# Postmix of an fp32 attention by 128 keys instead of 112: three whole parts a tile, half parts of two tiles side by side

## The chip, the cores and the metric

One core of one Trainium2 chip runs the whole program. The metric is the device time of one execution in microseconds. TensorE (PE; its weight loads are shown as PEld), VectorE (DVE), ScalarE (ACT), GpSimd (POOL) and SyncE (SP, which issues nearly all DMAs) run side by side and wait for each other by semaphores.

## What is computed

An attention over 4 batches, 12 heads, 448 tokens and 64 dimensions a head, whose heads are mixed before and after the softmax (premix by `w_pre`, postmix by `w_post`), and then two MLPs of 768 to 2048 to 768 over the 1792 tokens.

```python
scores = scale * np.matmul(q, k.transpose(0, 1, 3, 2))
scores = np.einsum('bhij,hg->bgij', scores, w_pre)
scores = scores - np.max(scores, axis=-1, keepdims=True)
attn = np.exp(scores)
attn = attn / (np.sum(attn, axis=-1, keepdims=True) + 1e-09)
attn = np.einsum('bhij,hg->bgij', attn, w_post)
return np.matmul(attn, v).astype(np.float32)
```

All of the attention is in fp32. Each fp32 matmul is two instructions on TensorE, each with a weight load of its own.

## The kernel before

The batches go in two groups of two: attention of a group, then both MLPs for it, then the other group. The MLPs split their operands in high and low fp32r parts and are not touched.

Within a group a batch's 448 rows of queries are 45 tiles of 10 rows (the last of 8), 90 tiles a group, in 8 chunks of 11 or 12 tiles. A tile has 10 rows times 12 heads = 120 rows of scores, by 448 keys. Two neighbouring tiles are a pair, and `slot(m)` writes out by hand the order of one pair's turn: 45 slots a group, each with the stages of several pairs:

- at its head, `keep(2m-1)` (the copy of the last pair's second tile), `soft(m+1)` (exponentials on ACT, L233), `premix(m+2)` (four matmuls on 64x64 quarters of the array, L217) and `top(m+2)` (maxima on DVE, L224);
- at its places A, B or C, up to three visits of `score` (L178, again 64x64 quarters), which are planned ahead of each chunk; some slots have none;
- `invert(m+1)` (reciprocals of the sums, DVE, L241 and L242), `postmix(2m)` with `keep(2m)`, `scale(m+1)` for both tiles (the post weights times the reciprocals, POOL, L251), in some slots `values` of a chunk (L293), then `postmix(2m+1)`.

`postmix(i)` takes the exponentials of a tile as weights, in JC = 4 parts of JP = 112 keys, and streams the scaled post weights `w2s` (12 heads times 10 rows = 120 columns). Its four results stand side by side in one bank, 112 partitions by 480 columns. `keep(i)` copies them into the chunk's tile `a` (keys, parts, heads, rows): even tiles on ACT (L278), odd tiles on DVE (L280). `values(c)` multiplies a chunk's `a` with V, over the same four parts, the two heads of a pair side by side: each matmul has 64 weight columns and writes one half of the output's partitions. The output banks `bo` are two, `w2s` tiles three, exponential tiles `p` four, `a` tiles two.

At the end of a group's slots `closing` runs the values of the last chunk. Beside the last ten slots of a group, steps of the next stage run on ACT, DVE and POOL (L585, L587 in the first group, L838, L842 in the second), and in the second group POOL also adds up weights (L492).

Of the kernel before, what the change touches and what calls it, by code (L numbers as in the profile page):

```python
# [7 lines left out]
F32 = mybir.dt.float32  # L8
# [8 lines left out]
RI = 10  # L17
# [51 lines left out]
def attention_mlp_kernel(ctx: ExitStack, tc, qT, kT, v, w_pre, w_post, mask, w1_in, w1_out, w2_in, w2_out, outT):  # L69
    nc = tc.nc  # L70
    B, _, _, S = kT.shape
    H, D = 2 * kT.shape[1], kT.shape[2] // 2
    JC, JP = v.shape[1], v.shape[2]
    DM = H * D
    P = 128
    KC = DM // P
    NF = w1_in.shape[0]
    G = H
    CH = chunks_of(S)
    CN = max(n for _, n, _, _ in CH)  # L80
# [16 lines left out]
    def bank(tag, name):  # L97
        return ps.tile([128, 512], F32, tag=tag, name=name)
# [5 lines left out]
    sh = ctx.enter_context(tc.tile_pool(name="sh", bufs=1))  # L104
# [25 lines left out]
    class Attention:  # L130
        def __init__(self, gi):
            self.gi = gi
            self.batches = list(range(gi * NB, gi * NB + NB))
            self.chunks = [(b, ci) for b in self.batches for ci in range(len(CH))]
            self.tiles, self.first, self.tb = [], [], []
            for c, (b, ci) in enumerate(self.chunks):
                r0, n, nt, nl = CH[ci]
                self.first.append(len(self.tiles))
                self.tiles += [(c, t, RI if t < nt else nl) for t in range(nt + (nl > 0))]
            self.first.append(len(self.tiles))  # L140
            self.n = -(-len(self.tiles) // 2)
            self.live, self.ss, self.aa, self.ap, self.xr = {}, {}, {}, None, None
            self.ks, self.n_raw, self.raw, self.at, self.late = None, 0, None, {}, False
            if gi == 0:
                self.first_opening()
            self.plan()
# [98 lines left out]
        def scale(self, m, a):  # L245
            if 2 * m + a >= len(self.tiles):
                return
            c, t, ni = self.tiles[2 * m + a]
            pts, rz = self.live["r", m]
            w2s = sh.tile([P, G * RI], F32, tag="w2s", name=f"w2s{self.gi}_{m}_{a}", bufs=3)  # L250
            nc.gpsimd.tensor_scalar(  # L251
                w2s[:, :G * ni].rearrange("p (g i) -> p g i", g=G), w2f[:, a, :, :ni], rz[:, a:a + 1], 1.0,
                op0=ALU.mult, op1=ALU.mult)
            self.live["w", 2 * m + a] = pts[a], w2s

        def postmix(self, i):
            if i >= len(self.tiles):
                return
            c, t, ni = self.tiles[i]
            pt, w2s = self.live.pop(("w", i))  # L260
            o = bank("bo", f"ps_o{self.gi}_{i}")
            for q in range(JC):
                nc.tensor.matmul(  # L263
                    o[:JP, q * G * ni:(q + 1) * G * ni], lhsT=pt[:, q * JP:(q + 1) * JP],
                    rhs=w2s[:, :G * ni], start=True, stop=True)
            self.live["o", i] = o

        def keep(self, i):
            if i >= len(self.tiles):
                return  # L270
            c, t, ni = self.tiles[i]
            if t == 0:
                self.aa[c] = self.ap.tile([JP, JC, G, CN], F32, tag="a", name=f"a{self.gi}_{c}", bufs=2)
            o = self.live.pop(("o", i))
            dst = self.aa[c].rearrange("p c g i -> p (c g) i")[:, :, t * RI:t * RI + ni]
            src = o[:JP, :JC * G * ni].rearrange("p (c i) -> p c i", i=ni)
            if i % 2 == 0:
                nc.scalar.activation(dst, src, AF.Copy)  # L278
            else:
                nc.vector.tensor_copy(dst, src)  # L280


        def values(self, c, vs, tag="bm"):
            b, ci = self.chunks[c]
            r0, n, _, _ = CH[ci]
            done = []
            for v in vs:
                xo = bank(tag, f"ps_v{self.gi}_{c}_{v}")
                for k in range(PAIRS):
                    for q in range(JC):  # L290
                        for e in range(2):
                            g = 2 * (v * PAIRS + k) + e
                            nc.tensor.matmul(  # L293
                                xo[e * D:(e + 1) * D, k * n:(k + 1) * n], lhsT=self.v[:, q, g, :],
                                rhs=self.aa[c][:, q, g, :n], start=(q == 0), stop=(q == JC - 1))
                done.append(xo)
            if self.xr is None:
                self.xr = sh.tile([P, KC, T], F32, tag="xr", name=f"xr{self.gi}")
            c0 = (b % NB) * S + r0
            for v, xo in zip(vs, done):  # L300
                dst = self.xr[:, v * PAIRS:(v + 1) * PAIRS, c0:c0 + n]
                src = xo[:, :PAIRS * n].rearrange("p (k i) -> p k i", i=n)
                nc.vector.tensor_copy(dst, src)
# [82 lines left out]
        def slot(self, m):  # L386
            work = self.at.get(m, [])

            def on(fn, k, *args):
                if 0 <= k < self.n:  # L390
                    fn(k, *args)

            def do(name, which=slice(None)):
                for fn, args in [w for w in work if w[0].__name__ == name][which]:
                    fn(*args)
            for k in self.fetches.get(m, ()):
                self.fetch(k)
            for name in ("fetch_k", "fetch_q", "fetch_v"):
                do(name)
            if 1 <= m <= self.n:  # L400
                self.keep(2 * m - 1)
            on(self.soft, m + 1)
            on(self.premix, m + 2)
            on(self.top, m + 2)
            visits = [w for w in work if w[0].__name__ == "score"]
            places = {0: "", 1: "B" if self.late else "A", 2: "BC" if self.late else "AC"}.get(
                len(visits), "AB" + "C" * len(visits))
            self.late = "C" in places

            def visit(place):  # L410
                for at, (fn, args) in zip(places, visits):
                    if at == place:
                        fn(*args)

            visit("A")
            on(self.invert, m + 1)
            if 0 <= m < self.n:
                self.postmix(2 * m)
                self.keep(2 * m)
            visit("B")  # L420
            on(self.scale, m + 1, 0)
            on(self.scale, m + 1, 1)
            for fn, args in work:
                if fn.__name__ == "values":
                    fn(*args, "by" if m % 2 else "bm")
            if 0 <= m < self.n:
                self.postmix(2 * m + 1)
                if m == self.n - 1:
                    self.keep(2 * m + 1)
            visit("C")  # L430

        def run(self, ap, behind, beside=None):

            self.ap = ap
            self.v = ap.tile([JP, JC, G, D], F32, tag="v", name=f"v{self.gi}")
            if self.gi == 0:
                for step in self.ahead():
                    step()
            behind, at = list(behind), self.n - 9
            for m in range(self.n + 1):  # L440
                if m < self.n:
                    self.slot(m)
                if beside:
                    beside(ap, m)
                if at <= m < at + KC:
                    behind.pop(0)()
                for _ in range(2):
                    if m >= at + KC and len(behind) > 2 * (self.n - m) + 1:
                        behind.pop(0)()
            return behind  # L450
# [294 lines left out]
    class Blocks(Mlps):  # L745
# [122 lines left out]
        def beside(self, ap, i):  # L868

            j, o = (i - 1) // 4, (i - 1) % 4  # L870
            todo = self.beside_todo
            if i < 1:
                return
            if o == 3 and 2 <= j < len(todo) + 2:
                self.store_sums(j - 2)
            if o == 1 and j < len(todo):
                prepare(*todo[j], 0, [ap.tile([P, 2, HW], F32, tag=f"pr{r}", name=f"pr{r}_{j}", bufs=3) for r in range(2)])
            if 1 <= j <= len(todo):
                prepare(*todo[j - 1], 1, eng=nc.gpsimd, ks=(o,))
# [269 lines left out]
def layout(q, k, v, w_pre, w_post, moe_w_in, moe_w_out, moe2_w_in, moe2_w_out):  # L1149
# [3 lines left out]
    B, H, S, D = q.shape  # L1153
    P = 128
# [3 lines left out]
    for c, (r0, n, nt, nl) in enumerate(chunks):  # L1158
        for t in range(nt + (nl > 0)):
            ni = RI if t < nt else nl  # L1160
# [3 lines left out]
            qT[:, c, ..., t + STEP * np.arange(ni)] = part.transpose(4, 0, 3, 1, 2)  # L1164
    qT = qT.reshape(B, len(chunks), 2 * D, H // 2, P)
    kT = k.transpose(0, 1, 3, 2).reshape(B, H // 2, 2 * D, S)
    vn = v.transpose(0, 2, 1, 3).reshape(B, 4, S // 4, H * D)

    def w_in(w):
        m, n = w.shape  # L1170
# [17 lines left out]
    own, head, i = given  # L1188
    mask[own, i[own]] = 1.0
    own, head, i = made  # L1190
# [31 lines left out]
```

## Time and profile before

| | us |
|---|---|
| runs | 1317.9, 1318.53, 1320.31 (median 1318.53) |
| profiled execution | 1314.12, span 1312.2 |
| TensorE busy | 1291.6 (98% of the span) |
| DVE, ACT, POOL busy | 918.3, 653.8, 263.0 |
| granted TensorE clock, mean | 0.997 |
| attention stages | about 15 to 211 and 699 to 898 |

A share of busy time is an average over stages. Matmuls are pipelined and their ends are modelled, so the sequence of their starts says more than their busy time. In a row of the groups the numbers behind the first bar are busy us and mean ns of one, those behind the second the idle time before and what ended it.

### The profile page before, as it was taken

How to read it: one execution, taken by the hardware profiler on the slowest of the kernel's cores; microseconds unless marked ns; L12 is line 12 of the kernel's file. 1: busy time of each engine (PE TensorE's matmuls, PEld its weight loads, DVE VectorE, ACT ScalarE, POOL GpSimd, SP SyncE). 2: the span in 40 equal slices, each digit the busy share in tenths (PEclk: the TensorE clock that was granted, in tenths of full speed). 3: DMA queues.
4: the chain of work that ended last, by engine and by line, in shares of the span. 5: the costliest groups of instructions: out<-in, count | busy, mean ns of one | idle time of the engine just before them, and what ended most of it. 6: DMA issues, size and time to landing. Idle time of an engine off the chain costs nothing.

```text
span 1312.2 us, 23816 instructions
## 1 busy us (share of the span) xinstructions
PE 1291.6 (98%) x8788; PEld 1091.3 (83%) x8788; DVE 918.3 (70%) x1553; ACT 653.8 (50%) x1259; POOL 263.0 (20%) x346
## 2 busy tenths in 40 slices
PE   8999998999999999999999999999999999999998
PEld 3667677999999999998885676678999999999998
DVE  5665667777666688775555656664977896799975
ACT  4555554545322355542425545555768555446652
POOL 2111122343200033310101333351001120001422
PEclk9999999999999999999999999999999999999999
DMA  6633432766785576676775666676876856785432
GB/s 206 193 118 106 159 128 64 244 184 215 230 287 172 184 227 206 197 234 227 255 248 171 224 217 198 206 245 208 280 232 208 276 181 199 233 278 169 128 129 93
DMA packets 130803, 261.12 MB, mean 199 GB/s; under 512 B 13696, under 2 KB 99712, under 8 KB 130688
## 3 DMA queue, kind: packets, MB, share of 16 engines
q1 hardware_dynamic: 127232, 254.09, 60.1%
q10 hardware_dynamic: 3456, 5.51, 1.1%
q8 instruction: 70, 1.15, 0.4%
q14 instruction: 45, 0.37, 0.1%
HBM read 151.02 MB, written 69.99 MB: 168 GB/s over the span
## 4 chain that ended last, share of the span: by engine, by line
PE 95%; DVE 1%; DMA 1%; ACT 1%; SPq 1%; issue 0%; POOL 0%; ACTq 0%; POOLq 0%; DVEq 0%
PE ps_a L632 18%; PE ps_h L618 17%; PE ps_y L1020 16%; PE ps_w L920 15%; PE ps_o L263 12%; PE ps_m L217 6%; PE ps_s L178 6%; PE ps_v L293 5%; DMA k<-in_dram 0%; DMA wx<-low 0%; DVE mx L224 0%; DMA t<-s 0%; ACT xh L585 0%; SPq L791 0%; DVE arena L544 0%
## 5 line engine op out<-in xcount | busy, mean ns | idle before, releaser
L263 PEld LDWEIGHTS ps_o<-w2s,p 128*112 128x112 f32 x1440 | 155.4, 177 | 72.9 <-issue 36.3
L263 PE MATMUL ps_o<-w2s,p 128*112 128x120 f32 (+1 forms) x1440 | 176.7, 273 | 2.5 <-POOL w2s L251 2.5
L632 PE MATMUL ps_a<-gh,wh 128*128 128x448 f32 x384 | 141.4, 368 | 0.0
L632 PE MATMUL ps_a<-gh,wl 128*128 128x448 f32 x384 | 139.6, 363 | 0.0
L576 DVE TENSOR_TENSOR wl<-arena,wh 128x768 fp32r<-128x768 f32 x64 | 61.3, 958 | 111.1 <-ACT wh L575 106.0
L251 POOL TENSOR_SCALAR w2s<-w2f,rz 128x120 f32<-128x120 f32 x180 | 64.4, 370 | 333.3 <-DVE rz L242 258.0
L233 ACT ACTIVATE p<-ps_m,mx 128x448 f32<-128x448 f32 x180 | 111.9, 630 | 37.8 <-issue 36.1
L1009 POOL TENSOR_TENSOR o<-gi,o 128x448 fp32r<-128x448 f32 x28 | 55.5, 1986 | 346.8 <-ACT o L1004 232.5
L224 DVE TENSOR_REDUCE mx<-ps_m 128x1 f32<-128x448 f32 x180 | 103.9, 618 | 26.8 <-PE ps_m L217 26.8
L575 ACT ACTIVATE wh<-arena 128x768 fp32r<-128x768 f32 x64 | 53.8, 840 | 131.3 <-PE ps_a L632 115.8
L184 ACT ACTIVATE s<-ps_s 128x448 f32<-128x448 f32 x87 | 47.3, 544 | 123.9 <-PE ps_s L178 119.9
L1020 PE MATMUL ps_y<-o,wx 128*128 128x448 f32 x504 | 106.4, 364 | 0.0
L1020 PEld LDWEIGHTS ps_y<-o,wx 128*128 128x128 f32 x504 | 94.6, 188 | 7.1
L1020 PE MATMUL ps_y<-o,wh 128*128 128x448 f32 x336 | 99.9, 365 | 0.0
L610 POOL TENSOR_TENSOR gl<-g,gh 128x448 fp32r<-128x448 f32 x40 | 53.1, 1328 | 214.1 <-ACT gh L609 162.4
L217 PE MATMUL ps_m<-t,w1f 64*64 64x448 f32 x720 | 90.1, 557 | 1.8 <-issue 1.3
L632 PE MATMUL ps_a<-gl,wh 128*128 128x448 f32 x240 | 87.4, 364 | 0.0
L178 PE MATMUL ps_s<-k,q 64*64 64x448 f32 x672 | 80.9, 547 | 2.3 <-ACT s L184 2.3
L280 DVE COPY a<-ps_o 112x480 f32<-112x480 f32 (+1 forms) x90 | 58.7, 652 | 34.1 <-PE ps_o L263 34.1
L632 PEld LDWEIGHTS ps_a<-gh,wh 128*128 128x128 f32 x384 | 72.1, 188 | 10.9 <-issue 4.9
L293 PE MATMUL ps_v<-a,v 112*64 112x110 f32 (+1 forms) x1536 | 77.1, 260 | 1.5 <-DVE a L280 1.5
L293 PEld LDWEIGHTS ps_v<-a,v 112*64 112x64 f32 x1536 | 73.8, 137 | 5.7 <-ACT a L278 2.8
(110 smaller groups left out, 2872.7 us busy)
## 6 DMA issues: line engine op xcount, KB each, us to landing
arena<-in_dram SPq DMA_DIRECT2D x64, 768.0 KB
t<-s SPq DMA_DIRECT2D x176, 210.0 KB
keep<-arena SPq DMA_DIRECT2D x64, 384.0 KB
pr<-keep SPq DMA_DIRECT2D x88, 192.0 KB
wr<-sums_in SPq DMA_DIRECT2D x64, 192.0 KB
wr<-sums_out SPq DMA_DIRECT2D x64, 192.0 KB
low<-wl SPq DMA_DIRECT2D x28, 384.0 KB
wr<-keep SPq DMA_DIRECT2D x48, 192.0 KB
```

The source lines that it names most:

```text
L178: nc.tensor.matmul(out[e][to:to + half_p, :S], lhsT=q[own, to:to + half_p], rhs=keys[own], start=True, stop=True)
L217: nc.tensor.matmul(out[a][to:to + half_p, :S], lhsT=w1f[own], rhs=t[own], start=True, stop=True)
L224: nc.vector.reduce_max(mx[:, a:a + 1], o[:, :S], axis=AX.X, negate=True)
L233: nc.scalar.activation(pt, o[:, :S], AF.Exp, bias=mx[:, a:a + 1], accum_out=z[:, a:a + 1])
L251: nc.gpsimd.tensor_scalar(w2s[:, :G * ni].rearrange("p (g i) -> p g i", g=G), w2f[:, a, :, :ni], rz[:, a:a + 1], 1.0, op0=ALU.mult, op1=AL ...
L263: nc.tensor.matmul(o[:JP, q * G * ni:(q + 1) * G * ni], lhsT=pt[:, q * JP:(q + 1) * JP], rhs=w2s[:, :G * ni], start=True, stop=True)
L293: nc.tensor.matmul(xo[e * D:(e + 1) * D, k * n:(k + 1) * n], lhsT=self.v[:, q, g, :], rhs=self.aa[c][:, q, g, :n], start=(q == 0), stop=(q ...
L576: nc.vector.tensor_tensor(out=wl, in0=self.wr(n), in1=f(wh), op=ALU.subtract)
L618: nc.tensor.matmul(hp[:, :S], lhsT=lw[:, c * P:(c + 1) * P], rhs=rw[:, c, cols], start=(k == 0), stop=(k == 3 * KC - 1))
L632: nc.tensor.matmul(acc[d, e][:, :S], lhsT=lw[:, wc], rhs=rw[fc, e], start=(fc == 0 and k == 0), stop=(fc == NF - 1 and k == 2))
L920: nc.tensor.matmul(to[:, :S], lhsT=lw[:, wc], rhs=rw, start=(d == 0 and j == 0), stop=(d == DB - 1 and j == 2))
L1020: nc.tensor.matmul(self.acc[d][:, :S], lhsT=lw[:, wc], rhs=rw, start=(u == 0 and q == 0 and j == 0), stop=(u == NU // 2 - 1 and q == UF - ...
```

## The change

The 448 keys are cut in three parts of 128 and one of 64. `postmix` now makes the three whole parts of a tile (128 weight columns each). The 64-key parts of a pair's two tiles are made by a new step, `halves(m)`, behind `postmix(2m+1)`: the first tile's goes to partitions 0 to 63, the second's to partitions 64 to 127 of the second tile's bank, at columns 360 on. `keep` copies the three parts, and a new `keep_halves` copies each half (the even tile's on ACT, the odd tile's on DVE). The fourth part of `a` holds a tile's 64 keys in one half of its partitions and zeros in the other; for that `a` is two lasting tiles, whose fourth part POOL clears when the halves of its tiles change places (four times a group). V's last 64 keys are given twice, to both halves of its fourth part, so that the values can sum over all 128 partitions. There are four `w2s` tiles.

```diff
...
         def postmix(self, i):
             c, t, ni = self.tiles[i]
-            pt, w2s = self.live.pop(("w", i))
+            pt, w2s = self.live["w", i]
             o = bank("bo", f"ps_o{self.gi}_{i}")
-            for q in range(JC):
+            for q in range(JC - 1):
                 nc.tensor.matmul(
-                    o[:JP, q * G * ni:(q + 1) * G * ni], lhsT=pt[:, q * JP:(q + 1) * JP],
+                    o[:, q * G * ni:(q + 1) * G * ni], lhsT=pt[:, q * P:(q + 1) * P],
                     rhs=w2s[:, :G * ni], start=True, stop=True)
             self.live["o", i] = o
+        def halves(self, m):
+            o, at, half_p = self.live["o", 2 * m + 1], (JC - 1) * G * RI, P // 2
+            for a, i in enumerate(self.pair(m)):
+                ni = self.tiles[i][2]
+                pt, w2s = self.live.pop(("w", i))
+                nc.tensor.matmul(
+                    o[a * half_p:(a + 1) * half_p, at:at + G * ni], lhsT=pt[:, (JC - 1) * P:S],
+                    rhs=w2s[:, :G * ni], start=True, stop=True)
+
+        def place(self, i):
             c, t, ni = self.tiles[i]
             if t == 0:
-                self.aa[c] = self.ap.tile([JP, JC, G, CN], F32, tag="a", name=f"a{self.gi}_{c}", bufs=2)
+                n, odd = c % 2, self.first[c] % 2
+                if n not in self.ab:
+                    self.ab[n] = self.ap.tile([P, JC, G, CN], F32, tag="a", name=f"a{self.gi}_{n}", bufs=2)
+                if self.odd.get(n) != odd:
+                    self.odd[n] = odd
+                    nc.gpsimd.memset(self.ab[n][:, JC - 1], 0.0)
+            return self.ab[c % 2], slice(t * RI, t * RI + ni)
...
+        def keep(self, i):
+            a, cols = self.place(i)
+            o, ni, w = self.live["o", i], self.tiles[i][2], JC - 1
+            self.copy(i, a[:, :w].rearrange("p c g i -> p (c g) i")[:, :, cols],
+                      o[:, :w * G * ni].rearrange("p (c i) -> p c i", i=ni))
+
+        def keep_halves(self, m):
+            o, at, half_p = self.live["o", 2 * m + 1], (JC - 1) * G * RI, P // 2
+            for e, i in enumerate(self.pair(m)):
+                a, cols = self.place(i)
+                ni, own = self.tiles[i][2], slice(e * half_p, (e + 1) * half_p)
+                self.copy(i, a[own, JC - 1, :, cols], o[own, at:at + G * ni].rearrange("p (g i) -> p g i", i=ni))
+                self.live.pop(("o", i))
...
             if 1 <= m <= self.n:
                 self.keep(2 * m - 1)
+                self.keep_halves(m - 1)
...
                 self.postmix(2 * m + 1)
+                self.halves(m)
                 if m == self.n - 1:
                     self.keep(2 * m + 1)
+                    self.keep_halves(m)
...
-            self.v = ap.tile([JP, JC, G, D], F32, tag="v", name=f"v{self.gi}")
+            self.v = ap.tile([P, JC, G, D], F32, tag="v", name=f"v{self.gi}")
...
-    vn = v.transpose(0, 2, 1, 3).reshape(B, 4, S // 4, H * D)
+    vn = v.transpose(0, 2, 1, 3).reshape(B, S, H * D)
+    vn = np.concatenate([vn, vn[:, S - P // 2:]], axis=1).reshape(B, -1, P, H * D)
```

## Rows read from the trace of the kernel before

**Rows 1.** The page: the chain of work that ended last, its shares by line

```profile
PE ps_a L632 18%; PE ps_h L618 17%; PE ps_y L1020 16%; PE ps_w L920 15%; PE ps_o L263 12%; PE ps_m L217 6%; PE ps_s L178 6%; PE ps_v L293 5%; DMA k<-in_dram 0%; DMA wx<-low 0%; DVE mx L224 0%; DMA t<-s 0%; ACT xh L585 0%; SPq L791 0%; DVE arena L544 0%
```

**Rows 2.** Busy times by window, attention: us, engines' busy us (x instructions), clock, DMA

```profile
15.00:211.00 196.00, 191.84 (x2097) 133.46 (x2095) 124.25 (x285) 106.95 (x273) 35.44 (x93) 1.00 0.42 141
```

**Rows 3.** Timeline, TensorE: start, us to the last end, line, tile, shape, count

```profile
153.57 0.26 PE L293 MATMUL ps_v<-a,v 112*64 112x110 f32 x2
153.76 1.07 PE L263 MATMUL ps_o<-w2s,p 128*112 128x120 f32 x8
154.77 0.98 PE L178 MATMUL ps_s<-k,q 64*64 64x448 f32 x8
155.57 0.93 PE L217 MATMUL ps_m<-t,w1f 64*64 64x448 f32 x8
156.43 1.07 PE L263 MATMUL ps_o<-w2s,p 128*112 128x120 f32 x8
...
161.02 1.89 PE L263 MATMUL ps_o<-w2s,p 128*112 128x120 f32 x16
162.85 0.98 PE L217 MATMUL ps_m<-t,w1f 64*64 64x448 f32 x8
```

**Rows 4.** Timeline, TensorE: 5 of those 16; 3, then all 8 of 96 columns

```profile
161.02 0.77 PE L263 MATMUL ps_o<-w2s,p 128*112 128x120 f32 x5
...
890.79 0.50 PE L263 MATMUL ps_o<-w2s,p 128*112 128x96 f32 x3
...
890.79 1.00 PE L263 MATMUL ps_o<-w2s,p 128*112 128x96 f32 x8
```

**Rows 5.** Busy times by window, line L293 alone: us, PE, PEld, clock, DMA

```profile
51.76:56.43 4.67, 4.67 (x96) 4.53 (x96) 1.00 0.59 189
127.22:132.21 4.99, 4.99 (x96) 4.83 (x96) 1.00 0.21 39
```

**Rows 6.** Groups by line and form, weight loads: busy us, mean ns

```profile
L263 PEld LDWEIGHTS ps_o<-w2s,p 128*112 128x112 f32 x1440 | 155.4, 177 | 72.9 <-issue 36.3 <-POOL w2s L251 20.6 <-POOL pr L492 14.1
...
L1020 PEld LDWEIGHTS ps_y<-o,wx 128*128 128x128 f32 x504 | 94.6, 188 | 7.1
```

**Rows 7.** Groups by line and form, the copies out of the output banks

```profile
L280 DVE COPY a<-ps_o 112x480 f32<-112x480 f32 x88 | 57.6, 654 | 31.8 <-PE ps_o L263 31.8
...
L278 ACT ACTIVATE a<-ps_o 112x480 f32<-112x480 f32 x88 | 50.8, 577 | 43.9 <-PE ps_o L263 43.9
...
L280 DVE COPY a<-ps_o 112x384 f32<-112x384 f32 x2 | 1.1, 556 | 2.4 <-PE ps_o L263 2.4
L278 ACT ACTIVATE a<-ps_o 112x384 f32<-112x384 f32 x2 | 1.0, 495 | 0.8 <-PE ps_o L263 0.8
```

**Rows 8.** Timeline, a slot with scores: both scalings, and the postmix that uses them

```profile
162.59 0.70 POOL L251 TENSOR_SCALAR w2s<-w2f,rz 128x120 f32<-128x120 f32 x2 [3.26 <-DVE rz L242]
...
164.51 1.89 PE L263 MATMUL ps_o<-w2s,p 128*112 128x120 f32 x16
```

**Rows 9.** Timeline, a slot without scores: the same two

```profile
186.21 0.70 POOL L251 TENSOR_SCALAR w2s<-w2f,rz 128x120 f32<-128x120 f32 x2 [2.63 <-DVE rz L242]
...
186.64 1.90 PE L263 MATMUL ps_o<-w2s,p 128*112 128x120 f32 x16
```

**Rows 10.** Line L251, who waited for it: us, times

```profile
PEld ps_o L263: 20.6, 27
```

**Rows 11.** Timeline, end of the first stage: last copy, then the values

```profile
208.43 0.56 DVE L280 COPY a<-ps_o 112x384 f32<-112x384 f32 x1 [1.18 <-PE ps_o L263]
...
209.13 5.06 PE L293 MATMUL ps_v<-a,v 112*64 112x118 f32 x96 [0.74 <-DVE a L280]
```

**Rows 12.** DMA issues (V), and the timeline's clear on POOL

```profile
v<-in_dram SPq DMA_DIRECT2D x8, 672.0 KB
...
0.72 0.47 POOL L311 MEMSET idle<- 128x448 f32 x1 [0.29 <-POOLq L1210]
```

More of the change, by code (lines that the diff above doesn't have):

```diff
@@ L72, in attention_mlp_kernel @@
     H, D = 2 * kT.shape[1], kT.shape[2] // 2
-    JC, JP = v.shape[1], v.shape[2]
+    JC = v.shape[1]
     DM = H * D
@@ L140, in __init__ @@
             self.first.append(len(self.tiles))
-            self.n = -(-len(self.tiles) // 2)
-            self.live, self.ss, self.aa, self.ap, self.xr = {}, {}, {}, None, None
+            assert len(self.tiles) % 2 == 0
+            self.n = len(self.tiles) // 2
+            self.live, self.ss, self.ab, self.odd, self.ap, self.xr = {}, {}, {}, {}, None, None
             self.ks, self.n_raw, self.raw, self.at, self.late = None, 0, None, {}, False
@@ L249, in scale @@
             pts, rz = self.live["r", m]
-            w2s = sh.tile([P, G * RI], F32, tag="w2s", name=f"w2s{self.gi}_{m}_{a}", bufs=3)
+            w2s = sh.tile([P, G * RI], F32, tag="w2s", name=f"w2s{self.gi}_{m}_{a}", bufs=4)
             nc.gpsimd.tensor_scalar(
@@ L256, in postmix, with copy @@
         def postmix(self, i):
-            if i >= len(self.tiles):
-                return
             c, t, ni = self.tiles[i]
-            pt, w2s = self.live.pop(("w", i))
+            pt, w2s = self.live["w", i]
             o = bank("bo", f"ps_o{self.gi}_{i}")
-            for q in range(JC):
+            for q in range(JC - 1):
                 nc.tensor.matmul(
-                    o[:JP, q * G * ni:(q + 1) * G * ni], lhsT=pt[:, q * JP:(q + 1) * JP],
+                    o[:, q * G * ni:(q + 1) * G * ni], lhsT=pt[:, q * P:(q + 1) * P],
                     rhs=w2s[:, :G * ni], start=True, stop=True)
             self.live["o", i] = o
-        def keep(self, i):
-            if i >= len(self.tiles):
-                return
+        def halves(self, m):
[7 more added lines that the diff above has]
+        def place(self, i):
             c, t, ni = self.tiles[i]
             if t == 0:
-                self.aa[c] = self.ap.tile([JP, JC, G, CN], F32, tag="a", name=f"a{self.gi}_{c}", bufs=2)
-            o = self.live.pop(("o", i))
-            dst = self.aa[c].rearrange("p c g i -> p (c g) i")[:, :, t * RI:t * RI + ni]
-            src = o[:JP, :JC * G * ni].rearrange("p (c i) -> p c i", i=ni)
+                n, odd = c % 2, self.first[c] % 2
[5 more added lines that the diff above has]
+            return self.ab[c % 2], slice(t * RI, t * RI + ni)
+        def copy(self, i, dst, src):
             if i % 2 == 0:
@@ L294, in values @@
                                 xo[e * D:(e + 1) * D, k * n:(k + 1) * n], lhsT=self.v[:, q, g, :],
-                                rhs=self.aa[c][:, q, g, :n], start=(q == 0), stop=(q == JC - 1))
+                                rhs=self.ab[c % 2][:, q, g, :n], start=(q == 0), stop=(q == JC - 1))
                 done.append(xo)
```

## The prediction

> **What bounds the kernel now.** I read the chain of work that ended last first [rows 1]: TensorE carries it, and the postmix line L263 alone is 12% of the span. Then the busy times of the first attention stage [rows 2]: 191.84 of 196 us are TensorE's at full granted clock (2.4 GHz), while DVE has 124 and ACT 107. The second stage (699 to 900 us) looks the same. So an edit is worth there what it does to TensorE's sequence of starts, unless it makes an operand late. The rest of the span (the products L618, L632, L920, L1020) is not touched.
>
> Next the starts of TensorE's blocks [rows 3]. Each fp32 matmul is two instructions. A pair of tiles has 16 postmix instructions. Run together they take from 161.02 to 162.85, 1.83 us; one tile alone takes 1.01 us (153.76 to 154.77), and two alone 2.02. Within a block the step is (1.89-0.77)/11 = 0.102 us [rows 4]. That leaves 1.83 - 14x0.102 = 0.40 us for the first weights and the leaving of the block.
>
> Last, whether the 0.102 is the streaming of 120 columns or the loading of 112 weight columns. The values' matmuls say what a streamed column costs: 96 instructions in 48 side-by-side steps take 4.67 us with 110 columns and 4.99 us with 118 [rows 5], so 0.32/48/8 = 0.83 ns a column. The last tile of a batch streams 96 columns instead of 120; by streaming its step would fall by 0.020 to 0.082 us. It is (1.00-0.50)/5 = 0.100 [rows 4]. So with 96 columns something else holds the step, and what did not shrink is the weights, 112 columns wide.
>
> **Whole parts.** Per pair 16 instructions with 112 weight columns become 12 with 128. A weight load takes 177 ns at 112 columns and 188 at 128 [rows 6] (that row is another type of weights): 11 ns more. So I put the new step at 0.112 us, an estimate: 0.100+0.011 from these rows, or 0.100x128/112 = 0.114; from below it is 0.102, if the loads still fit under 120 columns. A pair then takes 0.40+0.01+10x0.112 = 1.53 instead of 1.83, **-0.30 us** (bounds -0.28 and -0.41). Tiles that stand apart give the same: 2x(0.41+4x0.112) = 1.72 for 2.02.
>
> **Half parts.** Four instructions of 64 weight columns, two side by side, as the values do. Two steps of 120x0.83 ns are 0.20 us. The rows of the 64x64 forms price the rest [rows 3]: scores followed by premix, the same form, take 0.80 us, which is 2x0.373 (448 columns at 0.83 ns) plus 0.05 for weights that could not be loaded ahead; premix followed by postmix, another form, takes 0.86 with its weights already loaded, so leaving for another form costs 0.11. The values, 64 columns wide, pay it too: their last two start at 153.57 and postmix at 153.76, 0.19 where a step of theirs is 0.097. Today a pair has one border between postmix (128x112) and the 64x64 forms; it stays. New is one from 128x64 to 64x64, a pair of forms that never meets in this trace. With the border's price the halves cost 0.20+0.05+0.11 = **+0.36**; without, +0.20, if premix's own first weights then load ahead as well. I take 0.36, since every change of form that the trace has pays it. On this the Trainium skill, TensorEngine Tiling (Array Packing), section Key Properties, says that a change of tiling mode drains TensorE, a change of tile inside a mode does not; 128x64 and 64x64 are different modes there. By that rule the change pays a drain for each pair of tiles and comes out slower on TensorE; without it, faster. The borders in this trace agree; the new one is not in it.
>
> TensorE's net is -0.30+0.36 = +0.06 a pair, by the unrounded starts nearer +0.05; 90 pairs give **+4.5 us** (bounds, from 0.112/0.114 and rounding, +3 to +7).
>
> **Copies out of the output banks.** A tile's copy of 480 columns becomes one of 360 and one of 120. From 480 and 384 columns [rows 7] DVE pays 1.02 ns a column (0.53+0.29 for 0.65 us) and ACT 0.85 (0.48+0.27 for 0.58): +0.17 us each a pair. They stand at the head of the next pair's work: ACT's half copy waits for the halves, and behind it stand the two exponentials of the next pair; DVE's stands after keep and before the maxima of premix, which wait for premix anyway. The exponentials also wait for p tiles that the halves now hold until the pair's end. Where a slot has score matmuls the cover is large: scaled weights end by about 162.95 and postmix wants them at 164.51 [rows 8]. Behind both attention halves of the run lie stretches without scores (180 to 207 and 862 to 890 us, two times nine slots of about 2.74 us), where also split work lies on ACT and DVE: there the first scaled weights end at about 186.57 and postmix starts at 186.64 [rows 9]; the weight loads were last released by them 27 times [rows 10]. About 14 of the 18 slots are that tight. At 0.16 each (the shorter keep gives a little back) I add **+2.2 us** (0 if the shorter keeps pay for all of it, 6 if both copies' 0.34 us count in all 18).
>
> **The rest.** At each stage's end the values wait for the last copy [rows 11]: 0.74 us idle after a copy of 0.56. Then the halves (about 0.15 us more to their end), a copy of 288 columns (0.45) and one of 96 (0.25) stand there: +0.45, twice, **+0.9** (0.6 to 1.5). V grows by a seventh from 8 loads of 672 KB [rows 12]; nothing waits for V's landing in the trace, so 0. POOL clears a third of a 128x1416 tile eight times, about 1.5 us by its clear of 448 columns in 0.47 [rows 12]; behind it stands the scaling, which waits for DVE with POOL idle 2.6 to 3.3 us before it [rows 8, 9]: 0; if it met a scaling, 1.5 us eight times at most. Four w2s tiles instead of three match their longer life: 0.
>
> **Sum.** 4.5+2.2+0.9 = +7.6 us. The profiled execution took 1314.12 us (span 1312.2); the runs shown lie at 1317.9 to 1320.31, median 1318.53. I give the time against the median: 1326; against the profiled execution it would be 1321.7.
>
> **Rivals.** (a) *The new border is free.* The halves cost 0.20 to 0.25: -0.05 to -0.10 a pair, -4.5 to -9 us, with the copies' +3 about -4: 1314.5. For it: scores and premix, both 64x64, follow each other without a gap, and 128x64 shares their column split. Against: all other changes of form pay.
> (b) *128 weight columns still load under 120 streamed ones.* Step 0.102: -0.11 a pair, -10 us, so 7.6-10 = -2.4: 1316. Against it is the 96-column tile's step.
> (c) *The half copies come in line.* ACT's half copy and DVE's keep read one bank. If they are kept apart, ACT starts 0.53 us later in each pair; in the scored slots the slack takes it, in the 18 tight ones up to 0.5 us is lost: +9 more, 1335. The Trainium skill, PSUM — Partial Sum Buffer, section PSUM bank collisions, asks for two engines never to be in one bank and quadrant at once; no row of before shows two such reads side by side.
> (d) *The halves do not overlap* (the change does not do what it says): two more steps of 0.10 a pair, +18: 1344. Against it, the values' instructions of the same form run two by two.
>
> **How the numbers follow.** The forecast case has 0.63 (1322 to 1333), (a) 0.16, (b) 0.07, (c) 0.10, (d) 0.04. The range takes in the forecast, (b), (c) and half of (a): 1314 to 1335. About 0.2%, 2.6 us, is what a measurement can tell here. Faster: most of (a) and half of (b), 0.16. Same: the rest of these and the low edge of the forecast, 0.15. Slower: 0.69.
>
> **What would show it.** In the profile after: postmix steps near 0.112 us (0.102 would be b); the halves' two starts some 7 to 10 ns apart (one step apart is d); from the second step of the halves to premix about 0.20 us (0.10 is a); TensorE's busy time in the two stages up by about 5 us; more weight loads released by the scaling in the two stretches without scores; last waits before the values of about 1.2 us. The prediction is wrong if the stages get shorter, or if they lengthen through idle TensorE in the scored slots.

## The result and the profile after

| | before | after |
|---|---|---|
| median of six runs | 1316.95 us | 1333.42 us |
| lowest to highest | 1313.4 to 1320.31 | 1332.09 to 1336.06 |
| profiled execution (span) | 1314.12 (1312.2) | 1333.5 (1331.7) |
| TensorE busy | 1291.6 | 1307.0 |

The changed kernel takes **1.0131 times** as long (95% interval 1.0114 to 1.0148): 16.5 us by the medians, 15 to 19.5 by the interval. It is slower, as forecast, inside the range and near its upper end: +7.6 us had been worked out, and 1333.4 lies above the band given to the forecast case (1322 to 1333) and closer to rival (c)'s 1335 than to 1326. The granted clock is 0.997 in both profiles.

The page after, the chain of work by line; it answers to [rows 1]:

```profile
PE ps_a L659 18%; PE ps_h L645 16%; PE ps_y L1047 15%; PE ps_w L947 15%; PE ps_o L262 10%; PE ps_s L179 6%; PE ps_v L317 5%; PE ps_m L218 5%; PE ps_o L272 2%; DVE a L291 1%; DMA low<-wl 1%; ACT p L234 0%; DMA wx<-low 0%; DMA q<-in_dram 0%; DVE mx L225 0%
```

Postmix went from 12% to 10% (L262) and the half parts came for 2% (L272). New in the chain is a copy: L291, on DVE, with 1% of the span.

TensorE's own sequence, from the timeline after (start, us to the modelled end, line, tiles, shape, count), answers to [rows 3]:

```profile
58.83 0.93 PE L179 MATMUL ps_s<-k,q 64*64 64x448 f32 x8
59.69 1.60 PE L262 MATMUL ps_o<-w2s,p 128*128 128x120 f32 x12
61.22 0.43 PE L272 MATMUL ps_o<-w2s,p 128*64 128x120 f32 x4
61.58 0.98 PE L218 MATMUL ps_m<-t,w1f 64*64 64x448 f32 x8
```

Twelve instructions from 59.69 to 61.22 are 1.53 us, the halves from there to premix 0.36: 1.89 a pair where [rows 3] has 1.83.

The copies out of the output banks and the new clear, groups by line and form; they answer to [rows 7] and the clear of [rows 12]:

```profile
L291 DVE COPY a<-ps_o 128x360 f32<-128x360 f32 x88 | 46.7, 530 | 19.1 <-PE ps_o L272 17.6
L289 ACT ACTIVATE a<-ps_o 128x360 f32<-128x360 f32 x88 | 41.4, 470 | 2.3 <-PE ps_o L262 1.9
L291 DVE COPY a<-ps_o 64x120 f32<-64x120 f32 x88 | 25.1, 286 | 35.5 <-ACT a L289 28.4 <-POOL a L284 7.1
L289 ACT ACTIVATE a<-ps_o 64x120 f32<-64x120 f32 x88 | 23.4, 266 | 122.8 <-DVE a L291 122.8
L284 POOL MEMSET a<- 128x1416 f32 x8 | 10.2, 1280 | 0.0
```

The durations are the forecast's (0.53 and 0.29 on DVE, 0.48 and 0.27 on ACT). The releasers are not: in [rows 7] every copy is released by postmix on TensorE. Here ACT's half copies are released by DVE's keep, and DVE's half copies by ACT's half copy.

The waits after say the same by line (engine and line, for whom, us in total, times, longest):

```profile
ACT a L289 <- DVE a L291: 125.2, 90, 5.9
...
POOL w2s L252 <- PE ps_o L272: 41.2, 15, 6.9
...
PEld ps_o L262 <- POOL w2s L252: 29.6, 38, 1.5
...
DVE a L291 <- ACT a L289: 29.0, 86, 0.4
```

Ninety pairs, ninety waits of ACT for DVE; then 86 waits of DVE for ACT, 29.0/86 = 0.34 us each. The weight loads were released by the scaling 38 times, against 27 in [rows 10].

How that looks in one slot without scores, the stretch of [rows 9] (timeline after, rows that matter here):

```profile
186.86 1.90 PE L262 MATMUL ps_o<-w2s,p 128*128 128x120 f32 x12
...
189.19 0.53 DVE L291 COPY a<-ps_o 128x360 f32<-128x360 f32 x1
...
189.76 0.27 ACT L289 ACTIVATE a<-ps_o 64x120 f32<-64x120 f32 x1 [0.32 <-DVE a L291]
189.93 0.62 ACT L234 ACTIVATE p<-ps_m,mx 128x448 f32<-128x448 f32 x1
189.96 1.41 PEld L262 LDWEIGHTS ps_o<-w2s,p 128*128 128x128 f32 x12 [0.70 <-POOL w2s L252]
189.96 1.60 PE L262 MATMUL ps_o<-w2s,p 128*128 128x120 f32 x12
190.06 0.29 DVE L291 COPY a<-ps_o 64x120 f32<-64x120 f32 x1 [0.33 <-ACT a L289]
190.38 1.16 DVE L225 TENSOR_REDUCE mx<-ps_m 128x1 f32<-128x448 f32 x2
```

Keep on DVE from 189.19 to 189.72, then ACT's half to 190.03, then DVE's half to 190.35. The three read one bank, and each starts behind the end of the one before. The exponentials (L234) stand behind the second, the maxima of the next premix (L225) behind the third. Between its copies DVE idles 0.33 us, so the two copies take 1.16 us from the first's start to the second's end, where one took 0.65. Here postmix follows postmix after 189.96 - 186.86 = 3.10 us. Before, the same slot (the pair that ends at the postmix of [rows 9], 186.64) took 2.83; its first postmix was

```profile
183.81 2.00 PE L263 MATMUL ps_o<-w2s,p 128*112 128x120 f32 x16
```

By stage, from the first postmix of a group to the first product of its MLP, the attention took 190.62 and 199.19 us before, 195.55 and 208.85 after: +4.9 and +9.7. Another 3.1 of the profiles' 19.5 us difference lie in the first group's MLPs (484.98 and 488.07), whose instructions are the same; in all profiles of this study they took between 485.0 and 489.3, so these 3 us are not put down to the change, and the comparisons below go by the medians.

### The profile page after: what moved, and what is told of

It is laid out like the page before. It is cut to its first block, busy times and chain, and to the rows that moved or that the text cites. A ratio compares the mean times of both kernels' runs of the same rounds, so it can differ in the third digit from the quotient of the medians.

```text
span 1331.7 us, 23794 instructions
## 1 busy us (share of the span) xinstructions
PE 1307.0 (98%) x8788; PEld 1085.1 (81%) x8788; DVE 933.0 (70%) x1643; ACT 656.0 (49%) x1349; POOL 272.7 (20%) x354
## 4 chain that ended last, share of the span: by engine, by line
PE 92%; DVE 3%; DMA 2%; ACT 2%; issue 1%; POOL 1%; SPq 0%; POOLq 0%; ACTq 0%; DVEq 0%
PE ps_a L659 18%; PE ps_h L645 16%; PE ps_y L1047 15%; PE ps_w L947 15%; PE ps_o L262 10%; PE ps_s L179 6%; PE ps_v L317 5%; PE ps_m L218 5%; PE ps_o L272 2%; DVE a L291 1%; DMA low<-wl 1%; ACT p L234 0%; DMA wx<-low 0%; DMA q<-in_dram 0%; DVE mx L225 0%
## 5 line engine op out<-in xcount | busy, mean ns | idle before, releaser
L262 PEld LDWEIGHTS ps_o<-w2s,p 128*128 128x128 f32 x1080 | 129.9, 191 | 78.2 <-issue 36.5
L262 PE MATMUL ps_o<-w2s,p 128*128 128x120 f32 x1080 | 152.1, 286 | 5.9 <-POOL w2s L252 3.8
L289 ACT ACTIVATE a<-ps_o 128x360 f32<-128x360 f32 (+2 forms) x180 | 66.1, 367 | 127.5 <-DVE a L291 125.2
L291 DVE COPY a<-ps_o 128x360 f32<-128x360 f32 (+1 forms) x180 | 73.3, 407 | 58.1 <-ACT a L289 29.0
L225 DVE TENSOR_REDUCE mx<-ps_m 128x1 f32<-128x448 f32 x180 | 104.2, 619 | 13.3 <-PE ps_m L218 10.7
L234 ACT ACTIVATE p<-ps_m,mx 128x448 f32<-128x448 f32 x180 | 110.6, 619 | 2.7 <-DMA outT_dram<-ot 1.9
L947 PE MATMUL ps_w<-b_x,wx 128*128 128x448 f32 x360 | 78.6, 368 | 0.1
```

The source lines that it names most:

```text
L225: nc.vector.reduce_max(mx[:, a:a + 1], o[:, :S], axis=AX.X, negate=True)
L234: nc.scalar.activation(pt, o[:, :S], AF.Exp, bias=mx[:, a:a + 1], accum_out=z[:, a:a + 1])
L262: nc.tensor.matmul(o[:, q * G * ni:(q + 1) * G * ni], lhsT=pt[:, q * P:(q + 1) * P], rhs=w2s[:, :G * ni], start=True, stop=True)
L947: nc.tensor.matmul(to[:, :S], lhsT=lw[:, wc], rhs=rw, start=(d == 0 and j == 0), stop=(d == DB - 1 and j == 2))
```

## The experiments

Two theories were set against each other. By the one, TensorE's sequence (+4.5) and the copies' longer work account for the time; by the other, rival (c), the copies of the half parts come one behind the other, because ACT and DVE then read the same bank.

**TensorE's sequence without the half copies.**

```diff
         def keep_halves(self, m):
...
-                self.copy(i, a[own, JC - 1, :, cols], o[own, at:at + G * ni].rearrange("p (g i) -> p g i", i=ni))
```

> The changed kernel without the copies of the half parts (the last 64 keys of every tile are computed but not taken into the values). TensorE's instructions stay all as they are. Theory A (TensorE's new sequence costs 0.060 us a pair, 5.4 us, and the other 11 us come from the half copies, which wait for DVE's and ACT's reads of the same bank): about 6 us over the kernel before, 1323 where before is 1317; TensorE's blocks 1.53 and 0.36 us as in the changed kernel, no waits of ACT's copies for DVE's. Rival C (the other 11 us come from something else: V's longer load, POOL's clears, the fourth w2s tile): still 14 to 16 us over before.

Measured: 1322.08 against 1315.57, 1.0046 (1.0027 to 1.0064), +6 us. TensorE's instructions are those of after, so about 6 of the 16.5 us are its sequence (with what two keeps of 360 columns cost or give back), and some 10 hang on the half copies, directly or by what waits for them. (This kernel leaves the last 64 keys out of the values.)

**The copies alone, on the kernel before.** TensorE's work is before's; the second tile's copy is cut in three, DVE, ACT, DVE, as after has it.

```diff
-            else:
-                nc.vector.tensor_copy(dst, src)
+                return
+            half_p, w = P // 2, (JC - 1) * G
+            nc.vector.tensor_copy(dst[:, :w], src[:, :w])
+            nc.scalar.activation(dst[:half_p, w:], src[:half_p, w:], AF.Copy)
+            nc.vector.tensor_copy(dst[half_p:, w:], src[half_p:, w:])
```

> The kernel before (four parts of 112 keys, TensorE's instructions untouched) with the second tile's copy cut in three as in the changed kernel: DVE the first three parts (360 columns), then ACT 64 partitions of the fourth (120 columns), then DVE its other 48 partitions, all from one bank. Theory A (about 10 of the 16.5 us are the copies taking turns, whatever TensorE does): 7 to 11 us slower than before, 1323 to 1327 where before is 1316. Rival B (what costs is only the length of the extra copies): 2 to 3 us, 1318 to 1319. Rival D (the copies hurt only together with the longer hold of the exponential and w2s tiles by the halves): 0 to 3 us.

Measured: 1322.07 against 1316.99, 1.0054 (1.0031 to 1.0077): +5 us by the medians, +7 by the ratio. So the copies cut in three cost time without any change on TensorE, at or just under the lower end of what the turns were given. Its waits show the same turns (columns as above; L281 is DVE's keep, L282 ACT's half, L283 DVE's half):

```profile
ACT a L282 <- DVE a L281: 105.0, 89, 5.7
...
DVE a L283 <- ACT a L282: 30.0, 90, 0.4
```

**ACT's half copy ahead of DVE's keep.** The same copies, in the order ACT half, DVE keep, DVE half, so that DVE's two run without a turn between them.

```diff
-                self.keep(2 * m - 1)
-                self.keep_halves(m - 1)
+                self.keep_last(m - 1)
...
+        def keep_last(self, m):
+            self.keep_half(m, 0)
+            self.keep(2 * m + 1)
+            self.keep_half(m, 1)
```

> The changed kernel with the three reads of the second tile's bank in another order: ACT's half copy first, then DVE's copy of the three whole parts, then DVE's half copy. The same work, the same bytes. Theory A (DVE stands idle about 0.33 us a pair between its two copies, because ACT's half copy must wait for the first and the second for ACT's): that idle time goes and the exponentials start about 0.5 us earlier; about 5 us of the 16.5 come back, 1328 where before is 1317. Rival B (it is the length of the extra copies, 0.17 us a pair on each engine, not their taking turns): no change, 1333.

Measured: 1328.84, 1.0102 (1.0082 to 1.0123); that is about 4 us under after, with the same instructions. The two intervals overlap; the table of slots below bears the gain out. A slot of its timeline:

```profile
185.63 0.43 PE L272 MATMUL ps_o<-w2s,p 128*64 128x120 f32 x4
185.98 0.98 PE L218 MATMUL ps_m<-t,w1f 64*64 64x448 f32 x8
186.13 0.27 ACT L289 ACTIVATE a<-ps_o 64x120 f32<-64x120 f32 x1
186.29 0.62 ACT L234 ACTIVATE p<-ps_m,mx 128x448 f32<-128x448 f32 x1
...
186.79 0.82 DVE L291 COPY a<-ps_o 128x360 f32<-128x360 f32 x2
186.90 0.62 ACT L234 ACTIVATE p<-ps_m,mx 128x448 f32<-128x448 f32 x1
187.08 1.60 PE L262 MATMUL ps_o<-w2s,p 128*128 128x120 f32 x12
```

ACT's half starts as soon as the halves are done, and DVE's two copies are one piece of 0.82 us.

**No halves at all.**

```diff
         def halves(self, m):
...
-                nc.tensor.matmul(
-                    o[a * half_p:(a + 1) * half_p, at:at + G * ni], lhsT=pt[:, (JC - 1) * P:S],
-                    rhs=w2s[:, :G * ni], start=True, stop=True)
```

> The changed kernel without the half parts' matmuls and their copies (the last 64 keys of every tile are left out). Measures what the halves cost on TensorE, border to premix included. Theory A: 0.356 us a pair, 32 us, less than the kernel without the half copies: 1291 where that is 1323, if the other engines can follow (0 to 6 us of that may stay as idle time in the slots without scores). If the border to premix cost nothing and the halves only their two steps, 0.20 to 0.25 us a pair, 18 to 23 us: 1300 to 1305.

Measured: 1294.14, 0.984 (0.981 to 0.987), 27.9 us under the first experiment: 0.31 us for each of 90 pairs. That is near the price of the halves with their border (0.36 by the timeline), and too much for a free border (18 to 23 us). Pairs that follow each other after 3.55 us in the first experiment do so after 3.19 here, so the plain slots give the whole 0.36 back; of the 4.5 us missing from 90 times 0.36, 2.2 lie in the last nine slots of the groups. (This kernel leaves the last 64 keys out altogether.)

**The clears brought forward.** In the second group two of the clears hold the path. Timeline after:

```profile
738.33 1.00 POOL L519 TENSOR_TENSOR pr<-pr 128x384 f32<-128x384 f32 x1
...
739.27 1.27 POOL L284 MEMSET a<- 128x1416 f32 x1
...
739.33 0.93 PE L262 MATMUL ps_o<-w2s,p 128*128 128x120 f32 x6
...
740.29 0.47 ACT L289 ACTIVATE a<-ps_o 128x360 f32<-128x360 f32 x1
740.58 0.28 DVE L291 COPY a<-ps_o 64x120 f32<-64x120 f32 x1 [2.24 <-POOL a L284]
...
740.92 0.93 PE L262 MATMUL ps_o<-w2s,p 128*128 128x120 f32 x6 [0.66 <-DVE a L291]
```

The clear stands on POOL behind a weight sum (L519), DVE's half copy behind the clear, and the second tile's postmix behind that copy, which must free the bank. The pair's twelve instructions run from 739.33 to 741.78, 2.45 us instead of 1.53, and the maxima and scores behind that copy come late too: the next pair starts at 744.29, 4.97 us later, where such a slot takes 3.55. The same happens at 817.28 (4.98). In the first group the slot from 123.36 to 127.37 is longer by 0.46. The edit gives each clear a place of its own in the plan, some slots earlier.

```diff
+            for c in range(nch):
+                put(c if c < 2 else last[c - 2] + 3, self.clear, c)
```

> The changed kernel with POOL's clears of the fourth part brought forward: for the first two chunks in the first slots, for the others in the slot behind the values that read the tile last, instead of at the chunk's first copy. Theory: in the second attention stage two clears meet POOL's weight sums there, and postmix stands idle 0.92 and 0.93 us behind a copy that waits for the clear; these 1.8 us go, 1331 to 1332 where the changed kernel is 1333 (within what three rounds can tell; the idle times in the trace decide). Rival (the idle comes from the copies' order alone): they stay.

Measured: 1332.3, 1.0116 (1.0099 to 1.0133). In its timeline the same pair (the seventh of the group) is whole again, and the next one follows after 3.55:

```profile
741.95 1.60 PE L262 MATMUL ps_o<-w2s,p 128*128 128x120 f32 x12
743.48 0.43 PE L272 MATMUL ps_o<-w2s,p 128*64 128x120 f32 x4
```

The two idles, 0.92 and 0.93 us, are gone, and the three slots are 3.55 each: 0.46 + 1.42 + 1.43 = 3.3 us by the timeline. The time does not show them: the medians lie 1.1 us apart, which the intervals don't tell from nothing, and in this profile other slots are longer (two in the first group by 1.3 together, the first two of the second by 2.0). In the kernel without half copies the clears stand where they stand after, and the three slots take 3.55; so a clear costs only through the half copy that waits for it.

**Six `w2s` tiles.** After, 15 scalings were released by the halves, which hold their `w2s` to the pair's end (the waits above).

```diff
-            w2s = sh.tile([P, G * RI], F32, tag="w2s", name=f"w2s{self.gi}_{m}_{a}", bufs=4)
+            w2s = sh.tile([P, G * RI], F32, tag="w2s", name=f"w2s{self.gi}_{m}_{a}", bufs=6)
```

> The changed kernel with six w2s tiles instead of four and nothing else (in its trace POOL's scaling waits 15 times, 41 us in all, for the halves that still hold a w2s tile). Theory: what the copies alone (5 us) and TensorE's sequence alone (5 to 6 us) leave open of the 16.5 us is partly this longer hold, in the slots without scores: 1 to 3 us back, 1330 to 1332. Rival: where POOL waits for the tile the reciprocals are late anyway: no change, 1333.

Measured: 1332.56, 1.0125 (1.009 to 1.016), no difference from after. Those 41 us of waits lie beside the path.

**All parts 64 wide.** If what makes 128 keys dear is the weight load, and a border is paid only between forms, then each whole part as two matmuls of 64 weight columns, side by side in the output's halves, is the halves' own form throughout.

```diff
             for q in range(JC - 1):
-                nc.tensor.matmul(
-                    o[:, q * G * ni:(q + 1) * G * ni], lhsT=pt[:, q * P:(q + 1) * P],
-                    rhs=w2s[:, :G * ni], start=True, stop=True)
+                for e in range(2):
+                    nc.tensor.matmul(
+                        o[e * half_p:(e + 1) * half_p, q * G * ni:(q + 1) * G * ni],
+                        lhsT=pt[:, q * P + e * half_p:q * P + (e + 1) * half_p],
+                        rhs=w2s[:, :G * ni], start=True, stop=True)
```

> The changed kernel with each whole part of 128 keys made by two matmuls of 64 weight columns side by side, as the half parts are; results in the same places, copies as in the changed kernel. Theory A: then no instruction has 128 weight columns and the step is set by 120 streamed columns (0.1025 us for two side by side), and postmix and halves are of one form, so no border stands between them: a pair is 0.05+14x0.1025+0.10+0.095=1.68 at most (1.58 if the first loads hide) against 1.884 in the changed kernel and 1.824 before; -0.2 to -0.3 us a pair, -18 to -27 us on TensorE, of which the slots that are short of time on ACT and DVE give back some 5 to 10: 1310 to 1318 where the changed kernel is 1333. Rival (two loads of 64 columns take as long as one of 128, side by side or not): step 0.112, and only the border is gained: 14x0.112+0.15=1.72, about 1320 to 1325.

Measured: 1308.94, 0.9951 (0.9933 to 0.9969): faster than before. Its timeline:

```profile
58.13 1.45 PE L264 MATMUL ps_o<-w2s,p 128*64 128x120 f32 x24
59.41 0.38 PE L275 MATMUL ps_o<-w2s,p 128*64 128x120 f32 x4
59.71 0.98 PE L218 MATMUL ps_m<-t,w1f 64*64 64x448 f32 x8
```

Twenty-four instructions in 12 steps side by side take 1.28 us, the halves 0.30, a pair 1.58 instead of 1.89. The 0.31 times 90 are 28 us, of which 24 show.

**The same with ACT first, and with room.** First all parts 64 wide, with ACT's half copy ahead of DVE's keep as above:

> All parts in matmuls of 64 weight columns, and ACT's half copy ahead of DVE's copies. Theory A: the order gives about as much as it gave the changed kernel (3.8 us): 1304 to 1305 where the all-64 kernel is 1309 and before 1315.6; more if its shorter slots leave DVE less room, since DVE's idle 0.33 us a pair then counts in more slots. Rival B: no change against the all-64 kernel.

Measured: 1305.41, 0.9912 (0.988 to 0.9943), 3.5 us less by the medians, though the intervals overlap. Then also the early clears and six `w2s` tiles:

> The kernel with all parts of 64 weight columns and ACT first, and also the clears brought forward and six w2s tiles instead of four (in the all-64 kernel's trace POOL's scaling waits 20 times for the halves that hold a w2s tile, and two clears leave postmix idle 1.3 and 1.4 us). Theory A: another 3 to 5 us, 1299 to 1302; 1.1% faster than before. Rival: the scaling was not on the path and only the clears' 2.7 us come back.

Measured: **1298.16, 0.9861** (0.9843 to 0.9879), 19 us under the kernel before: the fastest version here.

**The same room for 128 wide parts.** ACT first, early clears, six `w2s` tiles, and postmix as after has it.

> The changed kernel with ACT's half copy first, the clears brought forward and six w2s tiles: all that was found beside TensorE's own sequence is eased, and that sequence (three parts of 128, halves side by side, 1.884 us a pair) stays. Against the all-64 kernel with the same three edits only the whole parts' form differs. Theory A (TensorE's sequence alone costs 5.4 us and nothing done beside it brings that back): 5 to 8 us over the kernel before, 1322 to 1325 where that is 1317. And 22 to 27 us over the all-64 kernel with the same edits (its pair takes 1.586 us, 0.298x90 = 26.8, less what the shorter slots leave idle). Rival (the copies were the whole loss): at or below before, 1315 to 1317.

Measured: 1326.89, 1.0072 (1.005 to 1.0093), +10 us, above the 5 to 8 expected. It differs from the one before only in the form of the whole parts, and lies 28.7 us above it; the pairs' 1.89 - 1.58 make 28. Its timeline still has tight slots:

```profile
184.69 0.43 PE L272 MATMUL ps_o<-w2s,p 128*64 128x120 f32 x4
185.04 0.98 PE L218 MATMUL ps_m<-t,w1f 64*64 64x448 f32 x8
...
185.96 0.74 PEld L262 LDWEIGHTS ps_o<-w2s,p 128*128 128x128 f32 x6 [0.70 <-POOL w2s L252]
185.96 1.89 PE L262 MATMUL ps_o<-w2s,p 128*128 128x120 f32 x12
```

Twelve instructions last 1.89 us here and 1.60 where they run together, and premix is followed by them 0.92 us later; ACT first does not give back all that the copies cost, though little of it is left (under 1 us, by the table below).

**Where the time lies, slot by slot.** A slot is here the time from a pair's first postmix to the next pair's. Of the 70 slots ahead of the last nine of each group, 62 are longer after than before by 0.05 to 0.08 us, which is TensorE's 0.06 and no more (3.55 for 3.49, 2.80 for 2.74): DVE and ACT take their turns there as well, and it costs nothing. The last nine slots of a group, and the first two of the second group, in us from the profiles:

| | last nine, first group | last nine, second group | first two, second group |
|---|---|---|---|
| before | 33.0 | 34.2 | 14.4 |
| after | 35.4 | 36.8 | 16.4 |
| without the half copies | 33.8 | 33.9 | 14.6 |
| the copies alone | 35.3 | 36.9 | 16.2 |
| ACT first | 34.1 | 34.8 | 18.4 |
| 128 wide with room | 34.2 | 34.9 | 16.3 |

After against before, the last nine cost 5.0 us, 1.1 of them TensorE's 0.06 a slot; 3.9 are left. The copies alone give 5.0. With ACT first, the same copies in another order, 3.3 of the 3.9 are gone: there it is the turns and not the copies' length that costs.

## Why the prediction was right in sign and half in size

**Whole parts: right.** Forecast a step of 0.112 us and 1.53 a pair; the timeline has 1.53, and six instructions end 0.93 us behind the first start (739.33), twelve 1.60 (59.69): 0.67/6 = 0.112. The streamed columns are 120 as before and the step grew with the weight columns, so the weight load sets it, as forecast; the groups by form after have

```profile
L262 PEld LDWEIGHTS ps_o<-w2s,p 128*128 128x128 f32 x1080 | 129.9, 191 | 78.2 <-issue 36.5 <-POOL w2s L252 29.6 <-POOL pr L519 8.5
```

with 191 ns for one, where [rows 6] gave 188 for another type of the same width. Rival (b) is excluded.

**Half parts: right.** Forecast 0.36 with the new border, measured 0.36: the first two start together, the second two 0.146 us later, premix 0.195 after those. Where two steps have one form, as in the version with all parts 64 wide, the halves follow postmix after 0.10. So a change from 128x64 to 64x64 is paid here by about 0.1 us, and rivals (a) and (d) fall. With this the trace agrees with the Trainium skill, TensorEngine Tiling (Array Packing), section Key Properties: a change of tiling mode drains TensorE, a change of tile within a mode does not.

**TensorE's net: right.** Forecast +4.5 (3 to 7); the pairs' starts give 0.06 x 90 = 5.4, the kernel without half copies +6 (3.6 to 8.4).

**Copies out of the output banks: the step that failed.** The term was put at +2.2, from the copies' longer durations alone, 0.16 us in each of about 14 slots. The durations were right. What was missing is that three copies of one bank take turns. I had that as rival (c), at 0.10, and as an alternative to the forecast; the turns are there in every pair and come on top, but cost time in the last nine slots of each group alone, much as (c) said (whether the second group's first two slots, below, belong to them stays open). There the term measured 3.9 us, and with ACT first, where the copies are as long but DVE's two run without a turn between them, 0.6: the length of the copies, from which I had the 2.2, costs 0.6 at most, and the turns the rest. The size that (c) gave them, 0.5 in each of 18 slots and +11 with my 2.2, was too much: 3.9 in 18 slots are 0.22 each (the slot shown is 3.10 - 2.83 = 0.27 longer, 0.06 of it TensorE's). That the shared bank and not the shared tile `a` makes the turns can be read above: at 740.29 and 740.58 ACT and DVE copy into the same `a` from two banks, and overlap; the same at 818.25 and 818.54; of the copies from one bank none overlap. The waits are semaphore waits. The Trainium skill, PSUM — Partial Sum Buffer, section PSUM bank collisions, keeps two engines from one bank and quadrant (32 partitions) at a time and allows different quadrants of a bank. By it keep and ACT's half must take turns; ACT's half (partitions 0 to 63) and DVE's (64 to 127) need not. The program's waits go beyond the rule: DVE waits there too, 0.34 us in each of 86 pairs. A kernel without that second wait was not tried, so whether its time can be had stays open.

**POOL's clears: put at 0, cost about 3.3 by the timeline.** This is the second step that failed. A clear takes 1.28 us, and the forecast's 1.5 was close; but I looked for a scaling behind it and found slack. What stands behind it is the half copy on DVE, and ahead of it a weight sum of the second group (L519, L492 before), which moves the clear into the path twice, at 1.4 us each; a third costs 0.46. All three slots have scores: idle TensorE there is what I had named as a sign against me. The bound that I gave, 1.5 in each of eight, contained it.

**The closings: put at +0.9, cost nothing beside the halves.** In [rows 11] the values start 0.74 us after TensorE's last work. After (timeline, end of the first stage):

```profile
213.22 0.42 PE L272 MATMUL ps_o<-w2s,p 128*64 128x120 f32 x4
213.69 0.46 DVE L291 COPY a<-ps_o 128x288 f32<-128x288 f32 x1 [1.43 <-PE ps_o L272]
...
214.29 1.43 PE L317 MATMUL ps_v<-a,v 128*64 128x118 f32 x24 [0.66 <-DVE a L291]
214.48 0.26 DVE L291 COPY a<-ps_o 64x96 f32<-64x96 f32 x1 [0.33 <-ACT a L289]
```

the idle is 0.66: the values start on the whole parts, and the half copies, from 214.18 on, end under them. I had let them wait for all. The +0.45 for each stage was also more than its pieces make: 0.15 + 0.45 + 0.25 for a copy of 0.56 are +0.29.

**V and the `w2s` tiles: 0, right.** No wait for V stands in the waits, and six tiles change nothing.

**The sum.** By the slots of the profiles: TensorE 5.4, the turns 3.9, the clears 3.3, the second group's first two slots 2.0 (16.4 for 14.4, without TensorE's 0.12). That is 14.6, and the two stages differ by 4.9 + 9.7 = 14.6; the medians differ by 16.5 (15 to 19.5). The last term stood in no part of the forecast, and its cause stays open. In those two slots the exponentials wait 1.9 us for an output's DMA on ACT's queue. With one profile each, the slots take 14.6 without the half copies and 16.2 with the copies alone, but 18.4 with early clears or with ACT first, and 14.7 to 15.1 where all parts are 64 wide. So the range held in part by luck: it reached to 1335 for (c)'s turns, which cost 3.9 us instead of 11, and the clears and this term filled the difference.

## What to carry over

Before the shape of a matmul is changed, find what sets its step: here 128 weight columns in 0.112 us, dearer than 120 streamed ones, so that wider weights bought less than they seemed to, and two 64 wide parts side by side were cheaper (0.102 us for a step of both inside a block, and no border between whole and half parts). Cutting a result in pieces multiplies its readers: write down for each output bank which engines read it and in which order, and give the turns a price where the slots are short of time: here they stood in all 90 pairs and cost in 18 slots. A clear costs what waits for it, and that can be an engine two steps further on. A rival that can happen beside the forecast is not an alternative to it but a term of the sum.

## What the runs showed beyond that

That postmix in the halves' form beats the 112 key form as well was not expected: 1.58 us a pair against 1.83 in [rows 3], with 28 instructions instead of 16, since the 12 steps run at 0.1 us and two instructions share each. And a wait's sum says little of its price: ACT's 125 us for DVE's keep are the largest new row of the waits, and the order without them (ACT's copies then wait 80 us for the halves on TensorE) is worth 3 to 4 us.
